# Five loads fewer in a DMA-bound decode block: wq and w_up whole, w_o in two, w_down in three, the first K in 96 and 160 tokens

## The chip, the cores and the metric

The kernel runs on one core of a Trainium2 chip, with nothing on the other cores. Times are device microseconds (us) of that core for one execution. The kernel before takes 186.19 us (median of 6 runs, 186.12 to 186.24). Each later group of experiments was timed beside its own runs of the kernel before (186.27 and 186.26 us; beside the single run of e9, one of 186.51 us).

## The reference, cut to what matters

One decode step for two sequences: attention with a per-batch modulation, then a gated feed-forward block.

```python
mod = silu(c) @ w_mod                            # w_mod 640 x 3840
sa, ca, ga, sb, cb, gb = ...                     # six parts of mod
h = layernorm(x) * (1 + ca) + sa                 # x: 2 x 1 x 640
q = h @ wq                                       # wq 640 x 6144: 32 heads of 192
k, v = the last 1024 tokens of the caches        # 2 x 32 x 1024 x 192 each
o = softmax(q . k * 192**-0.5) . v               # one query per head
x = x + ga * (o @ wo)                            # wo 6144 x 640
h = layernorm(x) * (1 + cb) + sb
x = x + gb * ((gelu(h @ w_gate) * (h @ w_up)) @ w_down)   # 640 x 1536 and back
```

All inputs are bf16. Every weight and every K and V value is used for two rows of `x` at most, so the work is to bring 76.88 MB into the core once.

## The kernel before: the parts that matter

All large inputs go through one buffer, `arena`, in a fixed order on one queue (the sync engine's): w_mod, wq, K0, V0 first half, K1 first half, V0 second half, K1 second half, V1 first half, V1 second half, w_o, w_gate, w_up, w_down. (K0 is the K of batch 0; a "half" is 128 of the 256 tokens that each of 4 partitions per head holds.) A load is issued when its place in the buffer is free:

```python
def pump(*consumed):
    queue["done"].update(consumed)
    while queue["next"] < len(items):
        it = items[queue["next"]]
        if not all(x in queue["done"] for x in items[:n] if overlap(x, it)):
            break
        queue["ops"][it] = S.dma("sp", ..., writes=keys(it))   # waits for the last readers of that place
        queue["next"] += 1
```

`keys(it)` names the buffer in pieces of 128 elements, so the sync engine waits only for the instructions that read the very piece. The chain that this makes is: K1's second half goes where V0's first half was, so it waits for P*V on V0; V1's first half goes where K1's first half was, so it waits for the last chunk of that K.

K is worked off in chunks of 16 tokens. VectorE multiplies by q (`L504`, in the changed file `L506`), TensorE folds the products into PSUM (`L516`/`L518`), and VectorE sums two chunks at a time (`L523`/`L525`). After the last chunk come softmax, the masked weights `Em` and P*V (`L567`/`L569`):

```python
for c in range(j0 // JC, (j0 + w) // JC):
    d_mul(it, c)
    p_reduce(it, c)
    if c % 2 == 0 and c > 0 and ("S", b, c // 2 - 1) not in made:
        c_sum(b, c // 2 - 1)
pump(it)
...
if last:
    softmax(b)
```

Of the kernel before, what the change touches and what calls it, by code (L numbers as in the profile page):

```python
# [119 lines left out]
def bass_adaLN_cond__sliding_block_cached__geglu_ffn__decode_kernel(  # L120
# [15 lines left out]
    B, _, D = A_x.shape  # L136
    _, H, Sk, Dh = A_k_cache.shape
# [3 lines left out]
    KT = D // P  # L141
    NQ = H * Dh
    NR = 4
    DR = D // NR
    XQ = P // H
    J = W // XQ
# [3 lines left out]
    FR = 3  # L150
    FC = F // P
# [4 lines left out]
    JC = 16  # L156
# [6 lines left out]
    JE = 64  # L163
    SLOT = JE * Dh
    UNIT = 128
    K_SPLIT = [[(0, 64), (64, 64), (128, 128)], [(0, 128), (128, 128)]]
    V_SPLIT = [[(0, 128), (128, 128)], [(0, 128), (128, 128)]]
    assert all(sum(n for _, n in x) == J and all(n % JE == 0 for _, n in x) for x in K_SPLIT + V_SPLIT)
    WQ_SPLIT = [(0, 2), (2, 3)]
    WO_SPLIT = [(0, 28), (28, 17), (45, 3)]  # L170
    WU_SPLIT = [(0, 3), (3, 2)]
    WD_SPLIT = [(9, 3), (0, 5), (5, 3), (8, 1)]
    RB = 16
    RM = RB * (B - 1) + 1
    ZW = P + DD - 1
# [8 lines left out]
    with es:  # L184
        S = _Sched(nc, es)
# [4 lines left out]
        arena = sb("arena", [P, NAR], BF16)  # L190
        wq_n = [n * NQ for _, n in WQ_SPLIT]
        wo_n = [n * D for _, n in WO_SPLIT]
        place = {("wm", 0): (0, KT * 6 * D), ("wq", 0): (2 * SLOT, wq_n[0]), ("wq", 1): (2 * SLOT + wq_n[0], wq_n[1])}
        tiles = [("k", 0, 0, 5), ("k", 0, 1, 6), ("k", 0, 2, 0), ("v", 0, 0, 2), ("k", 1, 0, 4), ("v", 0, 1, 0), ("k", 1, 1, 2), ("v", 1, 0, 4), ("v", 1, 1, 0)]
        span = {}
        for kind, b, t, z in tiles:
            j0, n = (K_SPLIT if kind == "k" else V_SPLIT)[b][t]
            place[(kind, b, t)] = (z * SLOT, n * Dh)
            span[(kind, b, t)] = (j0, n)
        tiles = [it[:3] for it in tiles]  # L200
        place[("wo", 0)] = (2 * SLOT, wo_n[0])
        place[("wo", 1)] = (6 * SLOT, wo_n[1])
        place[("wo", 2)] = (2 * SLOT + wo_n[0], wo_n[2])
        o_g = 4 * SLOT
        o_u = o_g + KT * F
        o_d = o_u + KT * F
        place[("wg", 0)] = (o_g, KT * F)
        for i, (k0, nk) in enumerate(WU_SPLIT):
            place[("wu", i)] = (o_u + k0 * F, nk * F)
        for i, (r0, nr) in enumerate(WD_SPLIT):  # L210
            place[("wd", i)] = (o_d + r0 * D, nr * D)
# [48 lines left out]
        aR = sb("aR", [P, FT], BF16)  # L260
        selg = sb("selg", [P, NR, B], BF16)
        aT = sb("aT", [P, FC, RM], BF16)
        fin = sb("fin", [P, DR], F32)
        finb = sb("finb", [P, DR], BF16)
        ps = es.enter_context(nc.psum_tensor("ps", [P, 8, 512], F32))
# [8 lines left out]
        def bank(k):  # L274
            return ("bank", k)
# [28 lines left out]
        def source(it):  # L304
# [3 lines left out]
            if kind == "wq":  # L308
                k0, n = WQ_SPLIT[it[1]]
                return A_wq.rearrange("(p k) n -> p (k n)", k=KT)[:, k0 * NQ:(k0 + n) * NQ]  # L310
            if kind == "wo":
                t0, n = WO_SPLIT[it[1]]
                return A_wo.rearrange("(p t) n -> p (t n)", t=NT)[:, t0 * D:(t0 + n) * D]
            if kind == "wg":
                return B_w_gate.rearrange("(p k) n -> p (k n)", k=KT)
            if kind == "wu":
                k0, nk = WU_SPLIT[it[1]]
                return B_w_up.rearrange("(p k) n -> p (k n)", k=KT)[:, k0 * F:(k0 + nk) * F]
            if kind == "wd":
                r0, nr = WD_SPLIT[it[1]]  # L320
                return B_w_down.rearrange("(p r) n -> p (r n)", r=FC)[:, r0 * D:(r0 + nr) * D]
# [43 lines left out]
        for b in range(B):  # L365
            S.op("pool", lambda e, b=b: e.affine_select(out=selt[:, b, :].rearrange("p (i x) -> p i x", x=XQ),
                                                        in_=ones_b[:, 0:1].unsqueeze(2).broadcast_to([P, NR, XQ]),
# [4 lines left out]
                                                      in_=selt[:, b, :].rearrange("p (i x) -> p i x", x=XQ).unsqueeze(1).broadcast_to([P, HB, NR, XQ])),  # L372
# [51 lines left out]
        def ln_mod(tag, opc_idx, s_idx, dst_bf):  # L424
# [7 lines left out]
            def f(e):  # L432
                last = None
                hv = hrow[:, :].rearrange("p (m j) -> p m j", j=KT)
                for j in range(KT):
                    for i in range(NR):
# [9 lines left out]
                                            in_=mask_h[:, :].unsqueeze(1).broadcast_to([P, P // H, H])),  # L446
# [3 lines left out]
        for half in range(2):  # L450
            def f(e, half=half):
                last = None
                for k in range(KT):
                    wv = wm_v[:, k, :].rearrange("p (m i n) -> p m i n", i=NR, n=DR)
                    for i in range(NR):
                        last = e.matmul(ps[32 * i:32 * i + RM, half, 0:MH].rearrange("p (m n) -> p m n", n=DR), lhsT=scT[:, k, :],  # L456
                                        rhs=wv[:, 3 * half:3 * half + 3, i, :],
                                        start=(k == 0), stop=(k == KT - 1), tile_position=(0, 32 * i))
                return last
            S.op("pe", f, reads=["scT"] + keys(("wm", 0)), writes=[bank(half)], name="mod%d" % half)  # L460
            S.op("act", lambda e, half=half: e.activation(out=modR[:, 3 * half:3 * half + 3, :].rearrange("p m n -> p (m n)"),  # L461
                                                          in_=ps[:, half, 0:MH], func=ACTF.Copy),
# [6 lines left out]

        for w, (k0, nk) in enumerate(WQ_SPLIT):  # L470
            def f(e, w=w, k0=k0, nk=nk):
# [106 lines left out]
        for n, it in enumerate(tiles):  # L578
            kind, b, t = it
# [8 lines left out]
            last = j0 + w == J  # L588
# [15 lines left out]
        def p_sel(e):  # L604
            last = None
            for dd in range(DD):
                for jj in range(2):
# [7 lines left out]
                                           in_=ps[:, BK_OT, 0:B * NT].rearrange("p (b t) -> p b t", b=B), func=ACTF.Copy),  # L615
             reads=[bank(BK_OT)], writes=["oT"], name="oT")
        S.op("dve", lambda e: e.memset(ps[:, 0:4, :], 0.0), writes=[bank(z) for z in range(4)], name="init_W")
        NA = D - QW
        for ci, (t0, n) in enumerate(WO_SPLIT):
            def f(e, ci=ci, t0=t0, n=n):  # L620
# [33 lines left out]
        def ffn_gu(bk, wv, name, splits):  # L654
            for ci, (k0, nk, key) in enumerate(splits):
                def f(e, k0=k0, nk=nk):
                    last = None
                    for k in range(k0, k0 + nk):
                        wk = wv[:, k, :].rearrange("p (m i r) -> p i m r", i=NR, r=FR)
                        for i in range(NR):  # L660
                            last = e.matmul(ps[32 * i:32 * i + B, bk, 0:FT].rearrange("p (m r) -> p m r", r=FR), lhsT=h2T[:, k, :],  # L661
                                            rhs=wk[:, i, :, :], start=(k == 0), stop=(k == KT - 1), tile_position=(0, 32 * i))
                    return last
                S.op("pe", f, reads=["ln2_out"] + keys(key), writes=[bank(bk)], name="ffn_%s%d" % (name, ci))
# [3 lines left out]
             reads=[bank(0)], writes=["gl"], name="gelu")  # L668
        ffn_gu(1, wu_v, "up", [(k0, nk, ("wu", ci)) for ci, (k0, nk) in enumerate(WU_SPLIT)])
        S.op("dve", lambda e: e.tensor_tensor(out=aR[:, :], in0=ps[:, 1, 0:FT], in1=gl[:, :], op=ALU.mult),  # L670
             reads=[bank(1), "gl"], writes=["aR"], name="geglu")

        def a_T(e):
            last = None
            for i in range(NR):
                for r in range(FR):
                    c0 = 2 * (i * FR + r)
                    last = e.matmul(ps[:, 2, c0:c0 + B], lhsT=aR[:, :].rearrange("p (m r) -> p m r", r=FR)[:, :, r], rhs=selg[:, i, :],
                                    start=True, stop=True)
            return last  # L680
        S.op("pe", a_T, reads=["aR", "selg"], writes=[bank(2)], name="aT_T")
        S.op("dve", lambda e: e.tensor_copy(out=aT[:, :, 0:RM:RB], in_=ps[:, 2, 0:FC * B].rearrange("p (f b) -> p f b", b=B)),
             reads=[bank(2)], writes=["aT"], name="aT")
        for ci, (r0, nr) in enumerate(WD_SPLIT):
            def f(e, r0=r0, nr=nr):
                last = None
                for fc in range(r0, r0 + nr):
                    wv = wd_v[:, fc, :].rearrange("p (i n) -> p i n", i=NR)
                    for i in range(NR):
                        last = e.matmul(ps[32 * i:32 * i + RM, BK_OT, CY:CY + DR], lhsT=aT[:, fc, :], rhs=wv[:, i, :],  # L690
                                        start=(fc == WD_SPLIT[0][0]), stop=(fc == WD_SPLIT[-1][0]), tile_position=(0, 32 * i))
                return last
# [66 lines left out]
```

## Time and profile before

| what | value | view |
|---|---|---|
| span of the profiled execution | 185.0 us | head of the page |
| load queue | 97.2% of 16 engines' span, 76.88 MB | queue table |
| rate over the span | 416 GB/s | queue table |
| VectorE, TensorE busy | 58%, 58% | engine table |
| last w_down load landed | 182.12 us | completion increments |

The page's slices, two of its rows. Each digit is the DMA engines' mean busy share in one fortieth of the span (4.6 us), in tenths; below it is the rate in GB/s.

```profile
DMA  9989999999898989999998989899999999999990
GB/s 324 449 376 436 462 446 404 434 425 494 377 489 361 510 361 489 436 414 457 395 461 383 478 383 489 383 468 436 418 446 404 442 403 449 398 414 426 406 383 34
```

The reader is to see that there is no slice without DMA until the last: the kernel is bound by its loads. The queue table of the page (queue, packets, MB, share) says the same:

```profile
q1 hardware_dynamic: 3180, 76.88, 97.2%
HBM read 76.88 MB, written 0.00 MB: 416 GB/s over the span
```

The chain that ended last, in order of time (start, duration, what):

```profile
20.63 42.01 DMA arena<-in_A_k_cache_dram
...
84.66 0.43 DVE M L529
...
98.92 21.85 DMA arena<-in_A_k_cache_dram
...
155.23 26.50 DMA arena<-in_B_w_down_dram
181.73 0.04 issue
181.77 0.74 PE ps L690 x16
182.51 0.02 issue
182.54 0.34 DVE fin L695
182.87 0.02 issue
182.89 0.33 DVE finb L697
```

Its long pieces are loads. The last is w_down; 1.1 us of matmul and VectorE and then the store follow its last landing. The line at 84.66 us is the maximum over all scores of batch 0.

When the loads are issued is in the timeline of the sync queue (start, duration from the first issue to the last of a merged row, engine, line, operation):

```profile
83.40 0.54 SPq L283 DMA_DIRECT2D arena<-in_A_v_cache_dram  x1
98.92 0.54 SPq L283 DMA_DIRECT2D arena<-in_A_k_cache_dram  x1
114.98 6.68 SPq L283 DMA_DIRECT2D arena<-in_A_v_cache_dram  x2
134.69 2.00 SPq L283 DMA_DIRECT2D arena<-in_A_wo_dram  x3
```

When they land is in the trace too: a load is spread over 16 DMA engines, and each raises the load's semaphore by one when its share has landed. So each load has a first, a median and a last landing. K1's second half, issued at 98.92 us, had the load ahead of it still landing from 104.33 (first engine) to 106.24 us (last); V1's first half, issued at 114.98 us, from 118.85 to 120.77 us. I call the time from an issue to the first engine's landing of the load ahead its *lead*: 5.4 and 3.9 us here.

### The profile page before, as it was taken

Reading aid. Unit: us, or ns where it says so; the run is one execution under the profiler, and the core shown is the slowest. Engines: PE = TensorE matmul, PEld = TensorE weight load, DVE = VectorE, ACT = ScalarE, POOL = GpSimd, SP = SyncE. Lnnn points to the kernel's source line nnn. Section 1 sums busy time; section 2 is a strip of 40 time slices with the busy share of each in tenths; the row PEclk is TensorE's granted clock in tenths of the full one; section 3 lists DMA queues with packets and bytes.
Section 4 is the critical chain, followed back from the end, with each engine's and each line's share of the span. In section 5 each row is a group of like instructions: output and inputs, shape, how many; then the busy total and the mean of one; then the engine's idle time right before and its main releaser. Section 6 shows DMA issues by size and latency. Waiting matters only on the chain.

```text
span 185.0 us, 1611 instructions
## 1 busy us (share of the span) xinstructions
PE 107.2 (58%) x835; PEld 28.5 (15%) x558; DVE 106.7 (58%) x99; ACT 14.5 (8%) x27; POOL 6.5 (4%) x27
## 2 busy tenths in 40 slices
PE   0015720857766379662499565966662499715472
PEld 0011100040000000001252000600001266401231
DVE  6213000119699488965991999789975938202411
ACT  2032100140000000001000000010001000101610
POOL 7600000000000000000000000000000000000000
PEclk9999995555799966998559999999999569996576
DMA  9989999999898989999998989899999999999990
GB/s 324 449 376 436 462 446 404 434 425 494 377 489 361 510 361 489 436 414 457 395 461 383 478 383 489 383 468 436 418 446 404 442 403 449 398 414 426 406 383 34
DMA packets 3202, 76.97 MB, mean 416 GB/s; under 512 B 378, under 2 KB 508, under 8 KB 1148
## 3 DMA queue, kind: packets, MB, share of 16 engines
q1 hardware_dynamic: 3180, 76.88, 97.2%
q8 instruction: 5, 0.08, 0.2%
q10 hardware_dynamic: 16, 0.01, 0.0%
q14 instruction: 1, 0.01, 0.0%
HBM read 76.88 MB, written 0.00 MB: 416 GB/s over the span
## 4 chain that ended last, share of the span: by engine, by line
DMA 57%; DVE 24%; PE 16%; ACT 1%; issue 1%; SPq 1%
DMA arena<-in_A_k_cache_dram 35%; DMA arena<-in_B_w_down_dram 14%; DVE arena L504 14%; PE ps L567 9%; DMA arena<-in_w_mod_dram 8%; DVE S_sb L523 6%; PE ps L516 3%; DVE Em L553 2%; PE ps L456 2%; DVE negm L533 1%; ACT E_sb L541 1%; SPq L283 1%; PE ps L544 1%; PE ps L537 1%; DVE M L529 0%
## 5 line engine op out<-in xcount | busy, mean ns | idle before, releaser
L516 PE MATMUL ps<-arena,ident_b 128*128 128x512 bf16 x192 | 51.3, 412 | 25.8 <-DVE arena L504 25.8
L504 DVE TENSOR_TENSOR arena<-arena,qbc 128x3072 bf16<-128x3072 bf16 x32 | 54.8, 1750 | 8.3 <-DMA arena<-in_A_k_cache_dram 8.3
L567 PE MATMUL ps<-arena,Em 128*64 128x384 bf16 x256 | 26.6, 379 | 5.7 <-DVE Em L553 5.7
L523 DVE TENSOR_REDUCE S_sb<-ps 128x32 f32<-128x1024 f32 x16 | 19.5, 1218 | 10.1 <-PE ps L516 10.1
L567 PEld LDWEIGHTS ps<-arena,Em 128*64 128x64 bf16 x256 | 16.4, 128 | 31.0 <-DVE Em L553 22.2
L553 DVE TENSOR_TENSOR Em<-E_sb,maskE 128x2048 bf16<-128x2048 bf16 x8 | 18.0, 2283 | 3.4 <-PE ps L567 3.4
L478 PE MATMUL ps<-arena,hT 128*2 128x512 bf16 x60 | 6.7, 625 | 9.1 <-DMA arena<-in_A_wq_dram 8.1
L531 PEld LDWEIGHTS ps<-ident_f,M 128*1 128x1 f32 x2 | 0.2, 80 | 60.5 <-DVE M L529 60.5
L488 DVE CAST qrow<-ps 128x512 bf16<-128x512 f32 x1 | 0.7, 692 | 15.0 <-PE ps L478 15.0
L627 PE MATMUL ps<-arena,oT 128*2 128x512 bf16 (+1 forms) x96 | 4.0, 312 | 4.7 <-DMA arena<-in_A_wo_dram 4.7
L635 DVE COPY arena<-ps 128x128 f32<-128x128 f32 x1 | 0.3, 292 | 10.5 <-PE ps L627 10.5
L541 ACT ACTIVATE E_sb<-S_sb,nbias 128x256 bf16<-128x256 f32 x2 | 1.0, 508 | 65.8 <-DVE nbias L539 65.8
L574 ACT ACTIVATE On<-ps,rden 128x384 bf16<-128x384 f32 x2 | 1.2, 580 | 49.5 <-PE ps L567 49.5
L397 PE MATMUL ps<-ident_b,crow 2*128 2x2 bf16 x5 | 0.4, 177 | 7.9 <-DMA crow<-in_c_dram 7.9
L456 PE MATMUL ps<-arena,scT 128*17 128x480 bf16 x40 | 4.3, 597 | 0.7 <-DMA arena<-in_w_mod_dram 0.7
L410 PE MATMUL ps<-st,selstat 128*128 128x2 f32 x4 | 1.1, 348 | 6.1 <-ACT sqj L406 6.1
L402 DVE CAST X<-xr 128x160 f32<-128x160 bf16 x1 | 0.2, 245 | 6.4 <-DMA xr<-in_A_x_dram 6.4
L661 PE MATMUL ps<-arena,h2T 128*2 128x384 bf16 x40 | 3.6, 507 | 0.3 <-DVE h2T L441 0.3
L494 PE MATMUL ps<-qrow,selq 128*128 128x192 bf16 x16 | 2.7, 361 | 1.2 <-ACT qrow L485 1.2
L464 DVE TENSOR_SCALAR opc<-modR 128x160 f32<-128x160 f32 x2 | 0.5, 244 | 4.7 <-ACT modR L461 4.7
L437 PE MATMUL ps<-selrow,hrow 128*32 128x2 bf16 x40 | 0.7, 182 | 3.6 <-DVE hrow L428 3.6
L478 PEld LDWEIGHTS ps<-arena,hT 128*2 128x2 bf16 x20 | 0.6, 107 | 14.3 <-DMA arena<-in_A_wq_dram 9.9
(84 smaller groups left out, 52.8 us busy)
## 6 DMA issues: line engine op xcount, KB each, us to landing
arena<-in_A_v_cache_dram SPq DMA_DIRECT2D x4, 6144.0 KB, 25.8
arena<-in_A_k_cache_dram SPq DMA_DIRECT2D x3, 6144.0 KB, 39.2
arena<-in_A_k_cache_dram SPq DMA_DIRECT2D x2, 3072.0 KB, 42.5
arena<-in_w_mod_dram SPq DMA_DIRECT2D x1, 4800.0 KB, 14.2
arena<-in_A_wq_dram SPq DMA_DIRECT2D x1, 4608.0 KB, 31.2
arena<-in_A_wo_dram SPq DMA_DIRECT2D x1, 4480.0 KB, 25.8
arena<-in_A_wq_dram SPq DMA_DIRECT2D x1, 3072.0 KB, 20.7
arena<-in_A_wo_dram SPq DMA_DIRECT2D x1, 2720.0 KB, 31.9
```

Source lines behind the costliest of these rows:

```text
L283: return lambda e: e.dma_start(dst, src)
L456: last = e.matmul(ps[32 * i:32 * i + RM, half, 0:MH].rearrange("p (m n) -> p m n", n=DR), lhsT=scT[:, k, :], rhs=wv[:, 3 * half:3 * half + ...
L478: last = e.matmul(ps[32 * i:32 * i + B, n, :], lhsT=hT[:, k, :], rhs=wv[:, kk, i, n * QW:(n + 1) * QW], start=(k == 0), stop=(k == KT - 1) ...
L494: last = e.matmul(ps[:, BK_T + b, 0:Dh], lhsT=selq[:, b, u * P:(u + 1) * P], rhs=qrow[:, u * Dh:(u + 1) * Dh], start=(u == 0), stop=(u == ...
L504: S.op("dve", lambda e: e.tensor_tensor(out=kt, in0=kt, in1=qbc[:, b, :].unsqueeze(1).broadcast_to([P, JC, Dh]), op=ALU.mult), reads=[("qb ...
L516: last = e.matmul(o_ap, lhsT=ident_b[:, :], rhs=kt[:, :, t * GC:(t + 1) * GC], start=(t == 0), stop=(t == NCH - 1))
L523: S.op("dve", lambda e: e.tensor_reduce(out=S_sb[:, b, 2 * JC * pair:2 * JC * (pair + 1)], in_=ps[:, 2 * z:2 * z + 2, :].rearrange("p k (j ...
L541: S.op("act", lambda e: e.activation(out=E_sb[:, b, :], in_=S_sb[:, b, :], func=ACTF.Exp, scale=SCALE, bias=nbias[:, b:b + 1], accum_out=d ...
L553: S.op("dve", lambda e, z=z, j=j: e.tensor_tensor(out=Em[:, z, :, :], in0=E_sb[:, b, j:j + JE].unsqueeze(2).broadcast_to([P, JE, H]), in1= ...
L567: last = e.matmul(ps[64 * i:64 * i + 2 * H, BK_O, 0:ON], lhsT=Em[:, z, 2 * jp:2 * jp + 2, :].rearrange("p j h -> p (j h)"), rhs=view(it, l ...
L627: last = e.matmul(ps[32 * i:32 * i + B, bk, 0:w], lhsT=oT[:, t, :], rhs=wv[:, tl, lo:lo + w], start=(t < NR), stop=(t >= NT - NR), tile_po ...
L661: last = e.matmul(ps[32 * i:32 * i + B, bk, 0:FT].rearrange("p (m r) -> p m r", r=FR), lhsT=h2T[:, k, :], rhs=wk[:, i, :, :], start=(k == ...
```

## The change

The intent is fewer loads and so less cost per load. On the sync queue: wq and w_up whole, w_o in 39 + 9 row blocks, w_down in 8 + 3 + 1, and K0 in 96 + 160 tokens in place of 64 + 64 + 128. The buffer is laid out anew in steps of 32 tokens so that all of it fits. Nine of twelve small transposes before w_down are saved on the way. Apart from the order of w_down's parts (its last three row blocks came first before), the order of the work on TensorE and VectorE is otherwise the same.

```diff
-    K_SPLIT = [[(0, 64), (64, 64), (128, 128)], [(0, 128), (128, 128)]]
+    K_SPLIT = [[(0, 96), (96, 160)], [(0, 128), (128, 128)]]
     V_SPLIT = [[(0, 128), (128, 128)], [(0, 128), (128, 128)]]
-    WQ_SPLIT = [(0, 2), (2, 3)]
-    WO_SPLIT = [(0, 28), (28, 17), (45, 3)]
-    WU_SPLIT = [(0, 3), (3, 2)]
-    WD_SPLIT = [(9, 3), (0, 5), (5, 3), (8, 1)]
+    WQ_SPLIT = [(0, KT)]
+    WO_SPLIT = [(0, 39), (39, 9)]
+    WU_SPLIT = [(0, KT)]
+    WD_SPLIT = [(0, 8), (8, 3), (11, 1)]
 ... (buffer places; HS is half of the old SLOT of 64 tokens)
-        tiles = [("k", 0, 0, 5), ("k", 0, 1, 6), ("k", 0, 2, 0), ("v", 0, 0, 2), ("k", 1, 0, 4), ("v", 0, 1, 0), ("k", 1, 1, 2), ("v", 1, 0, 4), ("v", 1, 1, 0)]
+        tiles = [("k", 0, 0, 11), ("k", 0, 1, 0), ("v", 0, 0, 5), ("k", 1, 0, 9), ("v", 0, 1, 0), ("k", 1, 1, 5), ("v", 1, 0, 9), ("v", 1, 1, 0)]
 ... (a_T: three matmuls with an 8-column right side in place of twelve with 2)
```

More of the change, by code (lines that the diff above doesn't have):

```diff
@@ L165, in bass_adaLN_cond__sliding_block_cached__geglu_ffn__decode_kernel @@
     UNIT = 128
-    K_SPLIT = [[(0, 64), (64, 64), (128, 128)], [(0, 128), (128, 128)]]
+    K_SPLIT = [[(0, 96), (96, 160)], [(0, 128), (128, 128)]]
     V_SPLIT = [[(0, 128), (128, 128)], [(0, 128), (128, 128)]]
-    assert all(sum(n for _, n in x) == J and all(n % JE == 0 for _, n in x) for x in K_SPLIT + V_SPLIT)
-    WQ_SPLIT = [(0, 2), (2, 3)]
-    WO_SPLIT = [(0, 28), (28, 17), (45, 3)]
-    WU_SPLIT = [(0, 3), (3, 2)]
-    WD_SPLIT = [(9, 3), (0, 5), (5, 3), (8, 1)]
+    assert all(sum(n for _, n in x) == J for x in K_SPLIT + V_SPLIT)
+    assert all(n % (2 * JC) == 0 for x in K_SPLIT for _, n in x) and all(n % JE == 0 for x in V_SPLIT for _, n in x)
+    WQ_SPLIT = [(0, KT)]
+    WO_SPLIT = [(0, 39), (39, 9)]
+    WU_SPLIT = [(0, KT)]
+    WD_SPLIT = [(0, 8), (8, 3), (11, 1)]
     RB = 16
@@ L192, in bass_adaLN_cond__sliding_block_cached__geglu_ffn__decode_kernel @@
         wo_n = [n * D for _, n in WO_SPLIT]
-        place = {("wm", 0): (0, KT * 6 * D), ("wq", 0): (2 * SLOT, wq_n[0]), ("wq", 1): (2 * SLOT + wq_n[0], wq_n[1])}
-        tiles = [("k", 0, 0, 5), ("k", 0, 1, 6), ("k", 0, 2, 0), ("v", 0, 0, 2), ("k", 1, 0, 4), ("v", 0, 1, 0), ("k", 1, 1, 2), ("v", 1, 0, 4), ("v", 1, 1, 0)]
+        HS = SLOT // 2
+        place = {("wm", 0): (0, KT * 6 * D), ("wq", 0): (5 * HS, wq_n[0])}
+        tiles = [("k", 0, 0, 11), ("k", 0, 1, 0), ("v", 0, 0, 5), ("k", 1, 0, 9), ("v", 0, 1, 0), ("k", 1, 1, 5), ("v", 1, 0, 9), ("v", 1, 1, 0)]
         span = {}
@@ L197, in bass_adaLN_cond__sliding_block_cached__geglu_ffn__decode_kernel @@
             j0, n = (K_SPLIT if kind == "k" else V_SPLIT)[b][t]
-            place[(kind, b, t)] = (z * SLOT, n * Dh)
+            place[(kind, b, t)] = (z * HS, n * Dh)
             span[(kind, b, t)] = (j0, n)
         tiles = [it[:3] for it in tiles]
-        place[("wo", 0)] = (2 * SLOT, wo_n[0])
-        place[("wo", 1)] = (6 * SLOT, wo_n[1])
-        place[("wo", 2)] = (2 * SLOT + wo_n[0], wo_n[2])
-        o_g = 4 * SLOT
+        place[("wo", 0)] = (4 * HS, wo_n[0])
+        place[("wo", 1)] = (13 * HS, wo_n[1])
+        assert 4 * HS + wo_n[0] <= 9 * HS and wo_n[1] <= HS
+        o_g = 9 * HS
         o_u = o_g + KT * F
@@ L674, in a_T @@
             last = None
-            for i in range(NR):
-                for r in range(FR):
-                    c0 = 2 * (i * FR + r)
-                    last = e.matmul(ps[:, 2, c0:c0 + B], lhsT=aR[:, :].rearrange("p (m r) -> p m r", r=FR)[:, :, r], rhs=selg[:, i, :],
-                                    start=True, stop=True)
+            for r in range(FR):
+                last = e.matmul(ps[:, 2, NR * B * r:NR * B * (r + 1)], lhsT=aR[:, :].rearrange("p (m r) -> p m r", r=FR)[:, :, r],
+                                rhs=selg[:, :, :].rearrange("p i b -> p (i b)"), start=True, stop=True)
             return last
         S.op("pe", a_T, reads=["aR", "selg"], writes=[bank(2)], name="aT_T")
-        S.op("dve", lambda e: e.tensor_copy(out=aT[:, :, 0:RM:RB], in_=ps[:, 2, 0:FC * B].rearrange("p (f b) -> p f b", b=B)),
+        S.op("dve", lambda e: e.tensor_copy(out=aT[:, :, 0:RM:RB].rearrange("p (i r) b -> p i r b", r=FR),
+                                            in_=ps[:, 2, 0:FC * B].rearrange("p (r i b) -> p i r b", r=FR, i=NR)),
              reads=[bank(2)], writes=["aT"], name="aT")
```

## The prediction

> What bounds the kernel now: the DMA engines. The slice table shows DMA busy at 0.9 or more in almost every slice of the 185.0 us span; the queue table gives the load queue 97.2% of 16 engines' span for 76.88 MB (416 GB/s). The chain of waits is 57% DMA; its last long piece is the wait for w_down, 155.23 to 181.73 us, then 3.3 us of matmul, two VectorE operations and the store. VectorE and TensorE are 58% busy each. The packet records (a packet is one partition's row of a load) price a load: 49,152 B take 1.82 us, 3,840 B 0.149 us, 1,280 B 0.055 us: about 8 ns per packet plus 27.1 GB/s per engine (434 GB/s for 16). That agrees with the fabric ceiling in the Trainium skill, "DMA: Bandwidth & Descriptors", section "Where 436 GB/s comes from". Merging cannot speed up the bytes: 76.88 MB at that rate is 177 us.
>
> What the change removes: six loads. Each is 8 packets on each engine (8 x 8 ns) and one semaphore write (9 ns): about 75 ns, 0.45 us for six, all on the chain that ends last. The issues (0.33 to 0.54 us each) are off it. The page's "Measured" section puts a fixed time on each DMA, but queued loads here follow each other without gaps, so I count none of it. Nine tiny transposes before w_down go too: 0.47 us becomes about 0.2 us.
>
> What it moves.
> (a) wq lands whole, near 32.3 us; 60 matmuls follow instead of 36 (4.01 us), done near 39.0 instead of 36.5 us. K's first part (96 tokens) lands near 44.4 us, so this is hidden.
> (b) At K's second landing (62.6 us, unchanged) 160 tokens are left instead of 128: one more pair of chunks, 4.47 us by the timeline. Softmax, the first P*V and batch 1's K move back 4 to 4.5 us.
> (c) Loads waiting for these buffers are issued later: K1's second half at about 103 us (98.92 before), V1's first half at about 119 us (114.98). The queue before them drains at 104.3 to 106.2 us and 118.9 to 120.8 us (first and last engine). With about 1.0 us from issue to first packet, as at the trace's start, the faster engines run dry for up to 1.5 us at the second place, the slowest hardly: expected loss 0 to 0.4 us. V0's second half keeps its issue time (83.4 us).
> (d) Batch 1 ends 2.5 us later; the wait for w_o (4.25 us idle at 167.01) covers it.
> (e) w_up in one load: its 20 matmuls start near 177.2 us and end about 0.6 us later than now (178.45). w_down's 8+3+1 order leaves four matmuls after the last landing; TensorE should just keep up.
>
> Sum: -0.45 (packets) + 0.1 (queue running dry) + 0 (tail) = -0.35 us: 185.85 us, range 185.1 to 186.9. Chances: faster by over 2% 0.01, within 2% 0.97, slower by over 2% 0.02.
>
> It is seen so: the last w_down landing near 181.3 us on the chain (181.73 now); batch 0's softmax 4.5 us later; V1's first load issued near 119 us; DMA still 9 in the slices around 115 to 125 us. A gap there, or a tail after the last landing longer than 3.3 us, would show (c) or (e) wrong.
>
> What would make it wrong: a deeper gap at 119 us (up to 2 us) if P*V runs longer at the halved clock; an instruction fetch falling on the slowest DMA engine; a fixed cost per load that the packet records do not show, which would make the gain larger.

## The result, and the profile after

The changed kernel takes 188.00 us (6 runs, 187.51 to 188.41), the kernel before 186.19: a ratio of 1.0097, 95% interval 1.0079 to 1.0115. (A ratio is the mean time of one kernel's fast runs over the mean of the other's of the same rounds, so not quite the ratio of the medians quoted.) It is within 2% of before, but slower, and above the predicted range. Its runs also spread over 0.9 us, where those of before spread over 0.12 us.

The slices of the profiled execution (span 187.0 us, so 4.7 us each), and the queue table:

```profile
DMA  9999999999999899998989998999999999999980
GB/s 354 428 481 421 421 421 423 414 471 468 460 434 394 347 494 431 410 473 368 506 347 477 336 473 368 379 452 421 456 431 410 443 406 459 399 385 434 425 333 15
...
q1 hardware_dynamic: 2460, 76.88, 96.4%
HBM read 76.88 MB, written 0.00 MB: 411 GB/s over the span
```

The same bytes, 720 packets fewer, and no slice below 8 before the end. Yet 96.4% of 187.0 us is 180.3 us of engine time, more than 97.2% of 185.0, which is 179.8 us: for fewer packets the engines were busy longer. The chain:

```profile
20.44 41.79 DMA arena<-in_A_k_cache_dram
...
88.08 0.43 DVE M L531
...
154.80 28.91 DMA arena<-in_B_w_down_dram
183.71 0.04 issue
183.75 0.39 PE ps L691 x12
184.14 0.02 issue
184.16 0.34 PE ps L691 x4
184.50 0.02 issue
184.52 0.34 DVE fin L696
184.86 0.02 issue
184.88 0.32 DVE finb L698
```

The end still hangs on w_down, and the piece after the landing is as short as before. The wait for K1's second half (98.92 us in before) is gone from the chain: from 62 to 154 us the chain runs over VectorE and TensorE. The computation is now the one that is waited for, by the loads. The sync queue:

```profile
82.34 0.54 SPq L285 DMA_DIRECT2D arena<-in_A_v_cache_dram  x1
101.64 0.54 SPq L285 DMA_DIRECT2D arena<-in_A_k_cache_dram  x1
117.70 6.68 SPq L285 DMA_DIRECT2D arena<-in_A_v_cache_dram  x2
137.18 0.81 SPq L285 DMA_DIRECT2D arena<-in_A_wo_dram  x2
```

K1's second half is issued 2.7 us later and V1's first half 2.7 us later. Their leads shrink from 5.4 and 3.9 us to 2.45 (104.09 - 101.64) and 1.34 us (119.04 - 117.70). The landings (us: first engine, median engine, last engine):

| load | before | after | median moved by |
|---|---|---|---|
| V0 second half | 104.33, 104.67, 106.24 | 104.09, 104.40, 105.94 | -0.27 |
| K1 second half | 118.85, 119.20, 120.77 | 119.04, 119.51, 121.36 | +0.31 |
| V1 first half | 133.38, 133.79, 135.38 | 134.66, 135.23, 136.48 | +1.44 |
| V1 second half | 147.91, 148.32, 149.83 | 149.19, 149.77, 151.00 | +1.45 |
| w_down, last part | 180.23, 180.85, 182.12 | 181.32, 181.88, 184.11 | +1.03 |

Up to V0's second half the change gains its 0.3 us. The two loads with a short lead give back 0.6 and 1.1 us in the median. After them the loads follow without loss for the median engine, but the last engine falls from 1.2 us behind it (V1 second half) to 2.2 us (w_down). This second part of the loss, 1.0 us of the 2.0 by which the end moved, comes from two instruction fetches by the account below, which follows them.

The packet records show how the time is lost. Where a 49,152-byte packet takes 1.82 us, 31 packets that start between 102 and 110 us take longer by over 40 ns, the longest 3.54 us; so do 14 between 118 and 124 us. Together they are 0.78 us and 0.47 us for each of the 16 engines, in the mean. In the kernel before there is no such packet in these two stretches. Time without any packet comes to 0.4 us for each engine between 117 and 126 us (0.05 us between 102 and 112 us, and none in the kernel before). A stretched packet counts as busy: that is why the slices show 9 and the queue table shows more busy time.

### The profile page after: what moved, and what is told of

Same layout as the page of the kernel before. It is cut to its first block, busy times and chain, and to the rows that moved or that the text cites. A ratio compares the mean times of both kernels' runs of the same rounds, so it can differ in the third digit from the quotient of the medians.

```text
span 187.0 us, 1588 instructions
## 1 busy us (share of the span) xinstructions
PE 102.3 (55%) x826; PEld 26.4 (14%) x549; DVE 106.6 (57%) x99; ACT 14.5 (8%) x27; POOL 6.6 (4%) x27
## 3 DMA queue, kind: packets, MB, share of 16 engines
q1 hardware_dynamic: 2460, 76.88, 96.4%
## 4 chain that ended last, share of the span: by engine, by line
DMA 45%; DVE 36%; PE 16%; ACT 1%; issue 1%; SPq 0%
DMA arena<-in_A_k_cache_dram 22%; DVE arena L506 20%; DMA arena<-in_B_w_down_dram 15%; DVE S_sb L525 9%; PE ps L569 8%; DMA arena<-in_w_mod_dram 7%; DVE Em L555 5%; PE ps L518 4%; PE ps L458 2%; DVE negm L535 1%; ACT E_sb L543 1%; PE ps L546 1%; DVE M L531 0%; PE ps L539 0%; SPq L285 0%
## 5 line engine op out<-in xcount | busy, mean ns | idle before, releaser
L518 PE MATMUL ps<-arena,ident_b 128*128 128x512 bf16 x192 | 49.4, 402 | 28.8 <-DVE arena L506 28.8
L569 PE MATMUL ps<-arena,Em 128*64 128x384 bf16 x256 | 25.4, 366 | 5.7 <-DVE Em L555 5.7
L569 PEld LDWEIGHTS ps<-arena,Em 128*64 128x64 bf16 x256 | 15.8, 123 | 30.3 <-DVE Em L555 22.2
L480 PE MATMUL ps<-arena,hT 128*2 128x512 bf16 x60 | 6.0, 583 | 11.8 <-DMA arena<-in_A_wq_dram 11.8
L629 PE MATMUL ps<-arena,oT 128*2 128x512 bf16 (+1 forms) x96 | 5.3, 401 | 6.4 <-DMA arena<-in_A_wo_dram 6.4
L480 PEld LDWEIGHTS ps<-arena,hT 128*2 128x2 bf16 x20 | 0.7, 117 | 16.8 <-issue 16.8
L629 PEld LDWEIGHTS ps<-arena,oT 128*2 128x2 bf16 x48 | 1.5, 108 | 10.0 <-DMA arena<-in_A_wo_dram 6.5
```

Of the source, the lines that this page charges most:

```text
L480: last = e.matmul(ps[32 * i:32 * i + B, n, :], lhsT=hT[:, k, :], rhs=wv[:, kk, i, n * QW:(n + 1) * QW], start=(k == 0), stop=(k == KT - 1) ...
L518: last = e.matmul(o_ap, lhsT=ident_b[:, :], rhs=kt[:, :, t * GC:(t + 1) * GC], start=(t == 0), stop=(t == NCH - 1))
L569: last = e.matmul(ps[64 * i:64 * i + 2 * H, BK_O, 0:ON], lhsT=Em[:, z, 2 * jp:2 * jp + 2, :].rearrange("p j h -> p (j h)"), rhs=view(it, l ...
L629: last = e.matmul(ps[32 * i:32 * i + B, bk, 0:w], lhsT=oT[:, t, :], rhs=wv[:, tl, lo:lo + w], start=(t < NR), stop=(t >= NT - NR), tile_po ...
```

## The experiments

The theory (*late issue*): nothing about the merged loads is slow. K0's 160 tokens after the second landing make batch 0 end later; so two loads are issued with too short a lead, and their engines run dry or stretch packets. Rival 1: large rows or few loads cost bandwidth by themselves. Rival 2: the tail, where whole w_o, w_up and w_down must land before their matmuls start.

| kernel | median (range), us | ratio to before, 95% interval |
|---|---|---|
| after | 188.00 (187.51 to 188.41) | 1.0097, 1.0079 to 1.0115 |
| e1: K0 in three, other merges kept | 186.05 (185.84 to 186.27) | 0.9983, 0.9971 to 0.9995 |
| e2: K0 in two, nothing else | 188.76 (188.43 to 190.47) | 1.0150, 1.0118 to 1.0182 |
| e3b: before, one load held, lead 4.8 us | 186.27 (186.16 to 186.39) | 0.9994, 0.9980 to 1.0009 |
| e4: e1 with K0 in 128 + 128 | 189.14 (186.38 to 189.49) | inconclusive |
| e5: before, K1 second half held | 187.81 (186.42 to 188.21) | 1.0067, 1.0033 to 1.0100 |
| e6: before, V1 first half held | 187.92 (187.38 to 188.25) | 1.0083, 1.0064 to 1.0101 |
| e7: before, both held | 189.09 (188.32 to 189.21) | 1.0140, 1.0119 to 1.0160 |
| e8: after, the two late loads in halves | 186.02 (185.87 to 186.24) | 0.9987, 0.9973 to 1.0000 |
| e9: before, one load held until the queue is empty | 192.97 (one run) | one look |

### e1: K0 in three loads, all other merges kept

```diff
-    K_SPLIT = [[(0, 96), (96, 160)], [(0, 128), (128, 128)]]
-    WO_SPLIT = [(0, 39), (39, 9)]
+    K_SPLIT = [[(0, 64), (64, 64), (128, 128)], [(0, 128), (128, 128)]]
+    WO_SPLIT = [(0, 38), (38, 10)]     # and the places of before, wq at 4 * HS
```

> The changed kernel with K of batch 0 in three loads again (64, 64, 128 tokens); wq, w_o, w_up and w_down stay merged (w_o 38 + 10 rows, as the slots allow). Late-issue theory: K1's second half is issued near 99 us and V1's first near 115 us again, with 4 to 5 us of loads still queued, so no packet of theirs is stretched; five loads fewer than before at 75 ns each: 185.8 us (185.5 to 186.0). Rival 1, large rows or few loads cost bandwidth by themselves: 187 us or more, as four of the five merges are still there. Rival 2, the tail (w_o, w_up, w_down must land whole before their matmuls start): 187 us or more too.

Measured: 186.05 us, 0.17% below before; the best of all kernels here together with e8. The leads are 7.1 and 5.5 us. The sync queue and the end of the chain of e1:

```profile
97.13 0.53 SPq L285 DMA_DIRECT2D arena<-in_A_k_cache_dram  x1
113.19 6.68 SPq L285 DMA_DIRECT2D arena<-in_A_v_cache_dram  x2
...
156.02 25.38 DMA arena<-in_B_w_down_dram
181.40 0.04 issue
181.45 0.66 PE ps L691 x16
```

After the first 4 us only six packets are long by over 40 ns: five beside instruction fetches of 16,384 bytes (below) and one beside a fetch of 8,192 bytes at 87.61 us, which the kernel before has too (at 89.43 us). Four of the five merges are in, so four loads are saved (the expectation counts five). The last landing of w_down is at 181.78 us, 0.34 us earlier than before, against 0.30 us from four times 75 ns. The median engine landed 0.69 us earlier, so the match of the last one is partly luck. Rivals 1 and 2 fall for these four merges, and the price of a load in the prediction is of the right size.

### e2: K0 in two loads, nothing else changed

```diff
-    K_SPLIT = [[(0, 64), (64, 64), (128, 128)], [(0, 128), (128, 128)]]
+    K_SPLIT = [[(0, 96), (96, 160)], [(0, 128), (128, 128)]]   # in the places of after
```

> The kernel before with K of batch 0 in two loads (96 and 160 tokens) alone, in the slots that the changed kernel uses. Late-issue theory: the whole loss, less the gain of the other merges: 187.6 to 188.7 us, with issues near 102 and 118 us and stretched first packets of both loads. Rival 2 (tail of merged weights): 186.1 us. Rival 1 (large rows): between, some 186.5 us, as one load alone has 61,440-byte rows.

Measured: 188.76 us (the upper edge of what was expected is 188.7). The whole loss comes from this one split. The leads in its profile are 3.83 and 2.31 us:

```profile
100.32 0.54 SPq L286 DMA_DIRECT2D arena<-in_A_k_cache_dram  x1
116.38 6.68 SPq L286 DMA_DIRECT2D arena<-in_A_v_cache_dram  x2
```

Here the median engine lost almost nothing by the end (w_down's last part 180.74 us, before 180.85), but the last engine landed at 184.87 us, 4.1 us behind the median. It is 1.6 us behind at K1's second half (120.57 against 119.01 us), 2.6 us at V1's first half (136.34 against 133.77) and 4.2 us at w_o's first part (163.23 against 159.04), in which one of five instruction fetches (16,384 bytes, at 159.99 us) fell. It fell on this very engine: the packet that starts as the fetch ends (160.86 us) is stretched and ends at 162.73 us, where the last of the load's 16 semaphore records stands. The fetch and the stretch together are 1.4 us, so in this profile 1.4 of the 4.1 us are the fetch's. So the mean of the stretched packets is not the measure; the engine that comes last is.

### e3b: the kernel before, one load held a little

```diff
+            if (b, c) == (1, 1):                       # chunk 1 of batch 1's K reduced
+                queue["hold"][("k", 1, 1)] = [o]       # K1's second half depends on it
+                pump()
```

> The kernel before with one edit: the second half of batch 1's K is issued only when the second chunk of batch 1's K has been reduced, near 101.5 us in place of 98.9, some 2.8 us before the first engine is done with the queue. No load is larger, none is merged. Late-issue theory: its 16 first packets are stretched by 0.5 to 0.8 us in the mean, the median landing of that load and of all later ones moves by that: 186.7 to 187.1 us. Rivals 1 and 2: 186.2 us, nothing changes.

Measured: 186.27 us, no change, so the expectation failed. Its profile tells why: batch 0 was done earlier in this run (its maximum at 83.24 us; 84.66 in the profile of before), the second chunk with it, and the load was issued at 99.59 us with a lead of 4.8 us, not 2.8. There was no long packet around it. It is a point for the scale of leads: 4.8 us is enough.

### e4: K0 in 128 + 128 tokens

```diff
-    K_SPLIT = [[(0, 64), (64, 64), (128, 128)], ...]     # e1
+    K_SPLIT = [[(0, 128), (128, 128)], ...]
```

> As e1_k0_three, but K of batch 0 in two loads of 128 tokens: rows of 49,152 bytes as before, none larger. Late-issue theory: VectorE starts 7 us later on K and is still busy with the first half when the second lands (62.5 us), so batch 0 ends some 4 us later than before, and V0's second half, K1's second half and V1's first are all issued 3 to 5 us late: 188 to 190 us. Rival 1 in the form that 61,440-byte rows or 160 tokens after the last landing cost: 185.8 us.

Inconclusive. Two of the four runs (189.49 and 189.39 us, the profiled one among them) count as slow, because they are over 1.5% above this kernel's fastest; the two fast runs are 186.38 and 188.90 us. I draw nothing from it.

### e5, e6, e7: the issue times of the changed kernel in the kernel before

```diff
+            if (b, c) == (1, 2):  queue["hold"][("k", 1, 1)] = [o]; pump()      # e5 and e7
+                if (b, j) == (0, 128):  queue["hold"][("v", 1, 0)] = [o]; pump()  # e6 and e7, o: first half of that P*V
```

> The kernel before, the second half of batch 1's K held until the third chunk of batch 1's K has been reduced: issue near 101 us (clock high) to 103 us (clock low), 1.5 to 3.5 us before the first engine lands the load ahead of it (104.4 us); the hold before, at 4.8 us, did nothing. Late-issue theory: first packets of this load stretched, as in the changed kernel (2.45 us), mean loss up to 0.8 us per engine, and the last engine 0.3 to 1.0 us later at the end: 186.6 to 187.4 us. If only loads, sizes or the tail matter: 186.2 us.

> The kernel before, the first half of batch 1's V held until half of the P*V before it is done: issue near 116.4 to 118.4 us, 0.4 to 2.4 us before the first engine lands the load ahead of it (118.8 us), as in the changed kernel (1.34 us). Late-issue theory: some engines run dry, 0.5 to 1.5 us lost: 186.7 to 187.9 us. Otherwise 186.2 us.

> The kernel before with both holds: the issue times of the changed kernel with none of its merges. Late-issue theory: the sum of the two holds, 187.3 to 188.8 us, as the changed kernel (188.0) less the gain of its merges. Otherwise 186.2 us.

Measured: 187.81, 187.92 and 189.09 us. No load is merged or larger here, no computation is added, the tail is as before; a load is only issued later. One hold costs 0.7 to 0.8%, both cost 1.4%. (e5's median is above what was expected, e6's and e7's slightly.) e7's queue, with leads of 1.7 us (104.37 - 102.64) and 1.24 us (119.51 - 118.27):

```profile
102.64 0.54 SPq L283 DMA_DIRECT2D arena<-in_A_k_cache_dram  x1
118.27 3.13 SPq L283 DMA_DIRECT2D arena<-in_A_v_cache_dram  x2
```

This shows the cause by itself: a late issue of these two loads is enough for the loss, and more. No fetch adds to it here: the last engine is 2.5 us behind the median at V1's first half and 2.3 us at the end. The profiled run of e5 is its fastest (186.42 us; lead 3.1 us, eight long packets); its other three, of which there is no trace, took 187.76 to 188.21 us. The hold follows TensorE, whose clock differs from run to run, so I take the lead to differ too, but no trace of those runs shows it, and their mean granted clocks (0.872 in the fastest; 0.898, 0.907 and 0.831 in the others) do not settle it.

### e8: the changed kernel, its two late loads in halves

```diff
-    K_SPLIT = [[(0, 96), (96, 160)], [(0, 128), (128, 128)]]
-    V_SPLIT = [[(0, 128), (128, 128)], [(0, 128), (128, 128)]]
+    K_SPLIT = [[(0, 96), (96, 160)], [(0, 128), (128, 64), (192, 64)]]
+    V_SPLIT = [[(0, 128), (128, 128)], [(0, 64), (64, 64), (128, 128)]]
```

> The changed kernel, its computation as late as it is (K of batch 0 in 96 and 160 tokens), but the two loads that were issued late are cut in halves of 64 tokens, each issued as soon as its own half of the buffer is free: first halves near 97.5 and 110.5 us, over 6 us before the queue is empty. Two loads more (0.15 us). Late-issue theory: the loss goes though batch 0 still ends 3.3 us late: 185.9 to 186.2 us. If the later computation itself, the 61,440-byte rows or the tail cost the time: 187.5 us or more.

Measured: 186.02 us. The computation is as late as in the changed kernel (the maximum of batch 0 at 87.84 us), and K0 still has its 61,440-byte rows, but each half is issued when its own half of the buffer is free. The sync queue (merged rows: the first halves start them, at 98.62 and 108.34 us):

```profile
98.62 3.13 SPq L285 DMA_DIRECT2D arena<-in_A_k_cache_dram  x2
108.34 15.62 SPq L285 DMA_DIRECT2D arena<-in_A_v_cache_dram  x3
```

The leads are 5.5 us (104.09 - 98.62) and over 10 us (118.69 - 108.34), there is no group of long packets around them (as in e1, single ones beside fetches), and the loss is gone though two loads were added. So neither the later computation nor the long rows nor the new places in the buffer cost the time. What is left of rival 1 falls.

### e9: a load issued into an empty queue

```diff
+            if (b, c) == (1, 5):  queue["hold"][("k", 1, 1)] = [o]; pump()
```

> The kernel before, the second half of batch 1's K held until the sixth chunk of batch 1's K has been reduced: issue near 108.5 to 110.5 us, 2 us or more after the last engine has landed the load ahead of it (106.2 us). The engines stand still, so the trace gives the time from issue to the first packet of each engine by itself. If it is about 1.0 us on all engines, as for the first load of the program (my figure in the prediction), the load lands 14.5 + about 2 us after its issue, and the losses of the earlier holds (issue 2.5 us ahead of the end of the queue) need another cause. If it is 1.3 to 3.2 us, as the changed kernel's trace suggests, with stretched first packets, it lands 18 us or more after its issue and the engine fed last sets the end. Total about 190 to 192 us either way.

One look, 192.97 us. The load was issued at 109.03 us, after the last engine had landed the load ahead (106.19 us). The packet records of the 16 engines: the first packets start 1.33 to 2.01 us after the issue and take 1.92 to 2.74 us in place of 1.82; the second ones start 3.75 to 4.06 us after the issue. From there on every packet takes 1.82 us, and the load lands 16.8 to 17.2 us after its issue. The first packets fit the second alternative of the expectation; the landing (18 us or more was expected) and the total (190 to 192 us) do not. So an issue needs about 4 us until the engines are past the stretched first packet, of which 1.9 to 2.2 us are lost when nothing is queued (3.75 to 4.06, less 1.82 for one packet). The queue was empty here, so this is not quite the changed kernel's case, where the longest packets (3.54 us) were longer than any here (2.74 us). Why they stretch more while other packets still flow is open.

### All leads in one table

| kernel | lead of K1 second half, of V1 first half, us | last part of w_down: median, last engine, us | profiled run, us |
|---|---|---|---|
| before | 5.4, 3.9 | 180.85, 182.12 | 186.25 |
| e1 | 7.1, 5.5 | 180.16, 181.78 | 185.84 |
| e3b | 4.8, 5.9 | 180.69, 182.30 | 186.39 |
| e8 (first halves) | 5.5, 10.4 | 180.40, 181.84 | 185.91 |
| e5 | 3.1, 5.6 | 181.11, 182.28 | 186.42 |
| after | 2.45, 1.34 | 181.88, 184.11 | 188.23 |
| e6 | 6.8, 1.7 | 181.24, 183.92 | 187.98 |
| e2 | 3.8, 2.3 | 180.74, 184.87 | 188.94 |
| e7 | 1.7, 1.24 | 182.72, 185.04 | 189.16 |

Every profile with both leads of at least 3.9 us is at the floor (185.84 to 186.39 us); every profile with a lead of 2.45 us or less took 187.98 us or more. e5, with 3.1 us, lies at the floor too, but its K1 second half lost some 0.2 us in the median.

## Why the prediction was wrong, point by point

- *The bound, and the price of a load* were right. The loads bound the kernel, and e1, with four loads fewer, gained 0.32 us in time (0.17%; the interval of the ratio allows 0.1 to 0.5 us) against 0.30 us worked out. The count was wrong: five loads fewer, not six, so 0.38 us and not 0.45.
- *(a)* was right. wq was used up by 38.21 us (predicted 39.0), K0's first part landed at 44.09 us (44.4).
- *(b)* was right in kind: K0's second part landed at 62.23 us, and the maximum of batch 0 came 3.4 us later (88.08 after 84.66 us), where 4 to 4.5 were predicted. The profiles can't judge the size so finely: those with K0 in 64 + 64 + 128 have this maximum at 83.11 to 84.78 us, those with 96 + 160 at 87.68 to 88.08 us.
- *(c) is the step that failed*: "With about 1.0 us from issue to first packet, as at the trace's start, the faster engines run dry for up to 1.5 us at the second place, the slowest hardly: expected loss 0 to 0.4 us". The mechanism and the two loads were the right ones, and the issues came even earlier than foreseen (101.64 and 117.70 us, predicted 103 and 119). Two things were mis-sized. First, the start of a load: I counted until the first packet and took that packet to run at full speed. e9 shows 1.33 to 2.01 us to the first packet, which is then stretched, and 4 us until an engine is past it. In the changed kernel the time without a packet, 0.4 us for each engine, was at the upper end of what I expected; the stretched packets, which I had left out, are 1.25 us (0.78 + 0.47). The trace that I had showed such packets: of the program's first load 18 packets that start in the first 3.1 us take over 40 ns more than the usual 1.42 us, the longest 2.71 us. So K1's second half, with a lead of 2.45 us that I took to be safe, lost 0.6 us in the median, and V1's first half 1.1 us. Second, "the slowest hardly": I took the loss to fall on the engines that are ahead, which have 1.5 us to give. In the changed kernel the last landing of V1's first half itself came 1.1 us later (136.48 after 135.38 us). e2 shows that an engine can lose enough to become the last itself: one packet of V1's first half, which started at 120.03 us, before the last engine had landed the load ahead (120.57 us), took 3.22 us. Each packet of an engine starts within some ns of the end of the one before, so its seven next ones can be followed: they end at 135.95 us, where the last of the load's 16 semaphore records stands (it counts as landed at 136.34 us). The end waits for the last engine.
- *(d)* was right for the end: batch 1's softmax was later by 0.8 us (ACT started its exponentials at 143.37 after 142.55 us), and TensorE still sat idle for w_o (6.4 us before 166.70 us). Only the size was too high.
- *(e)* was right about the tail: from the last landing of w_down to the issue of the store it is 1.12 us (185.23 - 184.11), before 1.13 us (183.25 - 182.12). Its times came 2 us late with the rest of the queue: w_up landed at 179.30 us, where its matmuls were to start near 177.2; in e1 it landed at 177.14.
- *The test I gave for (c)*, a gap in the slices around 115 to 125 us, was blind. The slices there (112.2 to 126.2 us) read 8, 9 and 9, and there are eights all over the kernel before, because a stretched packet counts as busy and one slice averages 16 engines over 4.7 us. The landings of each load show it; the slices don't.
- The prediction's second rival, "an instruction fetch falling on the slowest DMA engine", is the rest of the loss in this profile. Each of the five fetches of 16,384 bytes stops one engine for about 1.0 us and stretches its next packets by 0.5 us in all. In the changed kernel the last engine's distance from the median grew from 1.2 to 2.1 us in w_o's first part, in which the fetch at 161.09 us fell; in the kernel before, the same fetch (160.87 us) left it at 1.5 us. The records don't name the engine, but it can be followed: the stretched packet at the end of the fetch (162.01 us) takes 2.34 us, the next one ends at 166.19 us, where the last of the load's 16 semaphore records stands; the last but one is at 165.40 us. The fetch at 180.54 us did the same to another engine, which became the very last. The last three landings of w_down are 183.06, 183.98 and 184.11 us, and the later two belong to these two engines. So an estimate without these two fetches is an end at 183.06 us, 0.9 us later than before in place of 2.0. Which engine a fetch hits is luck as far as these runs tell. No run took a fetch away, and the other five runs of the changed kernel have no trace; but the fastest of them (187.51 us) is still 1.3 us above before, and e7 loses more without a fetch on its last engine.
- The fixed time of a DMA stands in "DMA: Bandwidth & Descriptors", section "Anatomy of one DMA — SWDGE (gpsimd) path": some 2.0 us plus the bytes at 436 GB/s, for loads issued from GpSimd. For the 6.29 MB of e9, issued from the sync engine, that is an estimate of 16.4 us; the run shows 16.8 to 17.2 us. I counted none of it because queued loads hide it. That holds only while the lead is long enough, and the change had just cut the lead.

## What to carry to other kernels

In a kernel bound by its loads, fewer and larger loads gain only the small price of a load (75 ns here), while a larger piece at the wrong place moves the computation that frees the buffers, and with it the issue of later loads. Measure for each load how long the load ahead of it still has to run when it is issued; 3.9 us was enough here, 2.45 us was not, and 3.1 us (e5's profile) cost some 0.2 us. Where the lead is too short, cut the late load in two so that its first part can go as soon as its own part of the buffer is free: the extra load costs far less than the dry queue. The Trainium skill ("DMA: Bandwidth & Descriptors", "Rules for kernel authors") advises both to coalesce small transfers and to issue early; these runs agree with both (four merges, of loads of 160 KB and more, gained 0.17% in e1; one late issue lost 0.83% in e6), and show that the first can spoil the second.

## What the Trainium skill lacked or had wrong

- "DMA: Bandwidth & Descriptors", section "Latency and other measured facts", gives a first byte from the sync queue after about 600 ns. Here the first packet records of the 16 engines start 1.0 to 1.6 us after the start of the issuing instruction at the program's start, and 1.33 to 2.01 us after it in e9. From the end of that instruction (it takes 0.38 and 0.54 us) it is 0.6 to 1.3 and 0.8 to 1.5 us: the first engine is near the page's figure, and the page lacks that the last one is up to 0.9 us later.
- The same page lacks how far ahead a load has to be issued so that the queue does not slow down: with loads of 6.29 MB the profiles show no loss at a lead of 3.9 us and more, and 1.7 us and more above before at 2.45 us and less.
- The same page, section "Why a DMA increments its semaphore by 16 and not by 1", says that the engines finish independently. The runs agree and add a size: in every profile the last engine lands 0.4 to 1.0 us after the median in the loads before the first instruction fetch of 16,384 bytes, and 1.4 to 2.0 us after it in the load in which that fetch falls and in the next ones. So most of this distance is that of the engine which the fetch stopped, as far as the times tell. At the end of e2 it is 4.1 us.
- No page gives what an instruction fetch costs the loads (it belongs to "Runtime: NRT & Kernel Launch", section "Instruction fetch mechanics"): here five of 16,384 bytes per run, each about 1.0 us on one engine and 0.5 us more on its next packets, and up to 1.4 us at the end when they hit the last engine (e2).
- No page warns that a stretched packet counts as busy time (it belongs to "Perfetto Trace Analysis", section "DMA Engine Tracks"), so that a busy share of 9 tenths can hide 0.8 us lost by each engine in the mean.
